# Linear attention and a balanced expert layer: rows of x made inside the first search, first weights asked by the number alone, receptances scaled from PSUM, a fixed order

## The chip, the cores and the metric

The kernel runs on one core of one Trainium2 chip. The metric is the device time in microseconds; the kernel before takes 471.56 us (median of three runs, 471.13 to 471.58). The profile is of one execution, with a span of 470.2 us from its first to its last instruction.

A core has five engines that run side by side and wait for each other by semaphores: TensorE (PE; its weight loads are shown as PEld), VectorE (DVE), ScalarE (ACT), GpSimd (POOL) and SyncE (SP), which here only issues transfers. TensorE writes to PSUM, from where the other engines fetch results.

## The reference

Two blocks follow one another. The first is a recurrent linear attention (batch 4, 8 heads, 768 steps, head size 48), the second a layer of 8 experts to which the 3072 tokens are assigned so that each expert gets exactly 384.

```python
for t in range(S):
    cur = einsum('bhd,bhe->bhde', u * kt, vt)
    y[:, :, t] = einsum('bhd,bhde->bhe', rt, state + cur)
    state = w[:, :, None] * state + einsum('bhd,bhe->bhde', kt, vt)
x = y.transpose(0, 2, 1, 3).reshape(B * S, H * D)          # 3072 rows of 384

logits = x @ w_gate                                        # 3072 x 8
for idx in argsort(-logits.flatten()):                     # best pairs first
    tok, e = idx // E, idx % E
    if assigned[tok] >= 0 or counts[e] >= cap: continue    # cap = 384
    assigned[tok] = e; counts[e] += 1
for e in range(E):
    out[mask_e] = relu(x[mask_e] @ w1[e]) @ w2[e]          # 384 -> 1024 -> 384
```

## The kernel before

Attention goes by 24 units: a batch and a chunk of 128 steps each, four batches side by side, six chunks in turn. Within a unit keys and receptances are scaled by powers of w, so that their products can be taken without a loop over steps. There are two arms: `attention_mild` for decays between 0.7 and 1.2, which a flag read at run time chooses and which the measured inputs take, and `attention_any` for all others.

```python
def scale(n):                                   # a unit: scaled keys, receptances, own term
    load(n + 3)
    kt, rt, vt = loaded.pop(n)
    ks, rs = kss[n % 4], rss[n % 2]
    nc.vector.tensor_mul(ks[:, :, 0:D], heads(kt), heads(wk))
    nc.vector.tensor_mul(rs[:, :, 0:D], heads(rt), heads(wr))
    rk = pool.tile([128, DX], F32, name="rk")
    nc.gpsimd.tensor_mul(rk, rt, kt)
    marks["rk"] = nc.gpsimd.tensor_mul(rk, rk, u_bc).ins
    ...
    nc.vector.tensor_reduce(out=dd, in_=heads(rk), axis=AX.X, op=ALU.add)
    for h in range(H):
        nc.scalar.activation(AT[:, h % 2, h // 2, :], ident, AF.Copy, scale=dd[:, h:h + 1])

def turn(n):                                    # both transposed on TensorE, fetched by ScalarE
    for a in range(HP): nc.tensor.transpose(kT_ps[:, a, :], pair(ks, a), ident)
    for a in range(HP): nc.tensor.transpose(rT_ps[:, a, :], pair(rs, a), ident)
    nc.scalar.copy(kT, kT_ps)
    nc.scalar.copy(rT, rT_ps)

def pairs(n):                                   # products of keys and receptances, masked into AT
    ...
def outputs(n):                                 # y from the state and from AT; the state's update
    ...
def rows(n):                                    # the unit's rows of x, turned back and written to HBM
    xr_ps = ps.tile([128, HP, 128], F32, name="xr_ps")
    for a in range(HP):
        nc.tensor.transpose(xr_ps[:, a, :], turned[n][:, a, :], ident)
    xt = pool.tile([128, DX], F32, name="xt", bufs=3)
    nc.vector.tensor_copy(heads(xt), xr_ps...)
    nc.sync.dma_start(x_dram[ts(b * C + c, 128), :], xt)

for n in range(N):                              # a scheduler decides the order on each engine
    if n + 2 < N: scale(n + 2)
    if n + 1 < N: turn(n + 1); pairs(n + 1)
    outputs(n)
    if n > 0: rows(n - 1)
    if n > 0 and n % B == 0: gate(n // B - 1)   # four units' logits
    ...
gate(C - 1)
rows(N - 1)
```

Then one expert after another is filled. `likely` guesses the level at which an expert is full: three times it counts how many tokens lie above 16 candidates (`count`), then it marks the tokens (`acc`), numbers them (`place`), lists them (`tokens`), and the rows are gathered from HBM. A flag says whether the guess holds; if not, a slow search (`surely`) does it again. The first expert's fill stands after the arms have joined, the others beside the expert before.

```python
def count(self, pool, m, prop, cand, digit_of):
    ind = ...                                   # VectorE: which tokens lie above which candidate
    for j in range(NT // G): nc.tensor.matmul(each, ind..., prop..., ...)
    tt(own, each, self.same, ALU.mult)          # VectorE
    nc.vector.tensor_reduce(out=cnt, ...)
    self.summed = tt(wide, digit_of..., cnt..., ALU.mult)
    nc.tensor.matmul(all_ps, self.ones_h, wide, start=True, stop=True)
    return all_ps

def fill(self, fetch):
    flag = self.likely(**out)
    tok, listed = self.tokens(out["place"])
    got = fetch(tok)                            # three gathers on GpSimd's queue
    found = nc.values_load(flag[0:1, 0:1], ...)
    with self.tc.If(found < 1):
        ...
    self.leave(out["fmax"], out["acc"])
    return out["fmax"], tok, got

def fetch(fmax, tok, xg, late=False):           # after fill: expert number, then its weights
    nc.vector.tensor_scalar(out=number, in0=fmax[0:1, :], ...)
    e = nc.values_load(number[0:1, 0:1], ...)
    nc.sync.dma_start(w1, moe_w1[ds(e, 1)]...)
    ...

ahead = fetch(*walk.fill(rows), late=True)
xT = turn(ahead[0], ahead[-1])                  # gathered rows turned; then w2 is asked
for n in range(E):
    ...
    hid = hidden(w1, xT)                        # h_ps: 24 matmuls of 384 columns, relu
    ...result(n, c, hid, w2, tok)               # o_ps, scattered to the output
```

Of the kernel before, what the change touches and what calls it, by code (L numbers as in the profile page):

```python
# [26 lines left out]
def attention_any(ctx, tc, r, k, v, w, u, wg, x_dram, LG, ident, walk):  # L27
# [16 lines left out]
    lpool = ctx.enter_context(tc.tile_pool(name="a_load", bufs=4))  # L44
    pool = ctx.enter_context(tc.tile_pool(name="a_work", bufs=2))
    ps_t = ctx.enter_context(tc.tile_pool(name="a_ps_t", bufs=2, space=PSUM))
    ps_g = ctx.enter_context(tc.tile_pool(name="a_ps_g", bufs=4, space=PSUM))
    ps_y = ctx.enter_context(tc.tile_pool(name="a_ps_y", bufs=1, space=PSUM))

    NB = 3  # L50
    kpads = [const.tile([128, H, PD], F32, name=f"kpad{i}") for i in range(NB)]
    rpads = [const.tile([128, H, PD], F32, name=f"rpad{i}") for i in range(NB)]
# [64 lines left out]
    ATs, Ks, Rs = [], [], []  # L117
    for i in range(2):
        AT = const.tile([128, H, T], F32, name=f"AT{i}")
        nc.vector.memset(AT, 0.0)  # L120
        ATs.append(AT)
        K = {h: const.tile([128, HP, T], F32, name=f"K{h}_{i}") for h in LEVELS[:-1]}
        R = {h: const.tile([128, HP, 2, PD], F32, name=f"R{h}_{i}") for h in LEVELS}
        for t in (*K.values(), *R.values()):
            nc.gpsimd.memset(t, 0.0)
        Ks.append(K)
        Rs.append(R)
# [137 lines left out]
    walk.constants()  # L265
# [8 lines left out]
    walk.guess(LG, AX.XY, ps_t.tile([128, 128], F32, name="most_ps", tag="t"), ident)  # L274


class Mild:
# [6 lines left out]
    def __init__(self, ctx, tc, r, k, v, w, u, wg, ident):  # L284
# [5 lines left out]
        P2 = 2 * PD  # L290
        E = wg.shape[1]
        M = T // 2
        L = M + 1
        self.tc, self.sources = tc, (k, r, v)
        const = self.const = ctx.enter_context(tc.tile_pool(name="m_const", bufs=1))
        self.lpool = ctx.enter_context(tc.tile_pool(name="m_load", bufs=5))
        self.units = [(b, c) for c in range(C) for b in range(B)]
        self.loaded = {}

        self.vts, self.kss, self.rss = (  # L300
            [const.tile([128, H, PD], F32, name=f"{name}{i}") for i in range(n)]
            for name, n in (("vt", 6), ("ks", 4), ("rs", 2)))
        for t in self.vts + self.kss + self.rss:
            nc.vector.memset(t[:, :, D:PD], 0.0)
        mask = const.tile([128, 128], F32, name="mask_f")
        make_upper_triangular(nc, mask, val=1.0, diag=False)
        self.mask = const.tile([128, 128], U8, name="mask")
        nc.gpsimd.tensor_copy(self.mask, mask)
# [5 lines left out]
        self.wg_sb = const.tile([128, HP, 32], F32, name="wg_sb")  # L314
        nc.vector.memset(self.wg_sb, 0.0)
        flat = w.rearrange("h d -> (h d)")
        wp = const.tile([P2, 8, HP], F32, name="wp")
        nc.vector.memset(wp[:, 0, :], 1.0)
        with nc.allow_non_contiguous_dma(reason="a row to the partitions"):
            for q in range(2):  # L320
                nc.scalar.dma_start(wp[q * PD:q * PD + D, 0, :], w.rearrange("(a q) d -> q d a", q=2)[q])
        row = const.tile([1, DX], F32, name="row")
        nc.sync.dma_start(row, flat.unsqueeze(0))
        self.u_bc = const.tile([128, DX], F32, name="u_bc")
        self.load(0)
        nc.scalar.dma_start(self.u_bc, u.rearrange("h d -> (h d)").partition_broadcast(128))
        for q in range(2):
            nc.scalar.dma_start(self.wg_sb[q * PD:q * PD + D, :, 0:E],
                                wg.rearrange("(a q d) e -> q d a e", q=2, d=D)[q])
        for n in range(1, 3):  # L330
            self.load(n)


        up = const.tile([P2, HP, M + 2], F32, name="up")
        ch = const.tile([P2, HP, T + 2], F32, name="ch")

        nc.vector.tensor_scalar(out=wp[:, 0, :], in0=wp[:, 0, :], scalar1=W_MIN, scalar2=W_MAX,
                                op0=ALU.max, op1=ALU.min)
        nc.vector.memset(up[:, :, 0:1], 1.0)
        nc.gpsimd.memset(ch[:, :, M:M + 1], 1.0)  # L340
        for j in range(7):
            n = 1 << j
            m = min(2 * n, M + 2) - n
            by = wp[:, j, :].unsqueeze(2).to_broadcast([P2, HP, m])
            nc.vector.tensor_mul(up[:, :, n:n + m], up[:, :, 0:m], by)
            m = min(2 * n, M + 1) - n
            by = wp[:, j, :].unsqueeze(2).to_broadcast([P2, HP, m])
            nc.gpsimd.tensor_mul(ch[:, :, L - n - m:L - n], ch[:, :, L - m:L], by)
            nc.vector.tensor_mul(wp[:, j + 1, :], wp[:, j, :], wp[:, j, :])
        nc.vector.reciprocal(ch[:, :, L:T + 2], up[:, :, 1:M + 2])  # L350

        turned = const.tile([P2, HP, T], F32, name="turned")
        nc.scalar.copy(turned, ch[:, :, T + 1:1:-1])
        self.wp, self.scales = wp, []
        with tc.tile_pool(name="m_ps", bufs=2, space=PSUM) as ps, ExitStack() as part:
            for name, t in (("wk", ch), ("wr", turned)):
                sc_ps = ps.tile([128, HP, P2], F32, name="sc_ps")
                for a in range(HP):
                    nc.tensor.transpose(sc_ps[:, a, :], t[:, a, 0:T], ident[0:P2, 0:P2])
                sc = const.tile([128, DX], F32, name=name)  # L360
                nc.scalar.copy(sc.rearrange("p (h d) -> p h d", h=H),
                               sc_ps.rearrange("p a (q d) -> p (a q) d", q=2)[:, :, 0:D])
                self.scales.append(sc)

            pool = part.enter_context(tc.tile_pool(name="mild", bufs=1))
            ge = pool.tile([1, DX], F32, name="ge")
            nc.vector.tensor_single_scalar(out=ge, in_=row, scalar=W_MIN, op=ALU.is_ge)
            both = pool.tile([1, DX], F32, name="both")
            nc.vector.scalar_tensor_tensor(out=both, in0=row, scalar=W_MAX, in1=ge, op0=ALU.is_le, op1=ALU.mult)
            flag = pool.tile([1, 1], I32, name="flag")  # L370
            nc.vector.tensor_reduce(out=flag, in_=both, axis=AX.X, op=ALU.min)
            self.holds = nc.values_load(flag[0:1, 0:1])

    def load(self, n):
        if n >= len(self.units):
            return
        b, c = self.units[n]
        tiles = []
        for name, src in zip(("kt", "rt", "vt"), self.sources):
            H, D = src.shape[1], src.shape[3]  # L380
            if name == "vt":
                t = self.vts[n % len(self.vts)]
                into = t[:, :, 0:D]
            else:
                t = self.lpool.tile([128, H * D], F32, name=name)
                into = t.rearrange("p (h d) -> p h d", h=H)
            self.tc.nc.sync.dma_start(into, src[b, :, ts(c, T), :].rearrange("h s d -> s h d"))
            tiles.append(t)
        self.loaded[n] = tiles


def attention_mild(ctx, tc, mild, r, k, v, w, u, wg, x_dram, LG, ident, walk):
# [19 lines left out]
    const = ctx.enter_context(tc.tile_pool(name="a_const", bufs=1))  # L412
    pool = ctx.enter_context(tc.tile_pool(name="a_work", bufs=2))
    ps = ctx.enter_context(tc.tile_pool(name="a_ps", bufs=1, space=PSUM))

    units, load, loaded = mild.units, mild.load, mild.loaded
    u_bc, wg_sb, wp = mild.u_bc, mild.wg_sb, mild.wp
    wk, wr = mild.scales
    halves = [slice(q * PD, q * PD + PD) for q in range(2)]
    kss, rss, mask, state = mild.kss, mild.rss, mild.mask, mild.state  # L420

    live, turned, marks = {}, {}, {}

    def heads(t):
        return t.rearrange("p (h d) -> p h d", h=H)

    def pair(t, a):
        return t[:, 2 * a:2 * a + 2, :].rearrange("p q d -> p (q d)")

    def scale(n):  # L430
        load(n + 3)
        kt, rt, vt = loaded.pop(n)
        ks, rs = kss[n % 4], rss[n % 2]
        nc.vector.tensor_mul(ks[:, :, 0:D], heads(kt), heads(wk))
        nc.vector.tensor_mul(rs[:, :, 0:D], heads(rt), heads(wr))

        rk = pool.tile([128, DX], F32, name="rk")
        nc.gpsimd.tensor_mul(rk, rt, kt)  # L438
        marks["rk"] = nc.gpsimd.tensor_mul(rk, rk, u_bc).ins  # L439
        dd = pool.tile([128, H], F32, name="dd")  # L440
        nc.vector.tensor_reduce(out=dd, in_=heads(rk), axis=AX.X, op=ALU.add)  # L441
        AT = pool.tile([128, 2, HP, T], F32, name="AT", bufs=3)
        for h in range(H):
            nc.scalar.activation(AT[:, h % 2, h // 2, :], ident, AF.Copy, scale=dd[:, h:h + 1])  # L444
        live[n] = dict(vt=vt, ks=ks, rs=rs, AT=AT)

    def turn(n):

        ks, rs = live[n]["ks"], live[n]["rs"]
        kT_ps = ps.tile([128, HP, T], F32, name="kT_ps")  # L450
        for a in range(HP):
            nc.tensor.transpose(kT_ps[:, a, :], pair(ks, a), ident)
# [87 lines left out]
    for n in range(N):  # L540
        if n + 2 < N:
            scale(n + 2)
# [4 lines left out]
        if n > 0:  # L547
            rows(n - 1)
# [607 lines left out]
```

## Time and profile before

| what | value |
|---|---|
| time, median of three runs | 471.56 us |
| span of the profiled run | 470.2 us |
| TensorE busy | 410.9 us (87%) |
| VectorE busy | 218.4 us (46%) |
| ScalarE busy | 153.3 us (33%) |
| GpSimd busy | 123.4 us (26%) |
| moved by DMA | 54.36 MB, mean 116 GB/s |
| rows of x turned (xr_ps) and written | 24 units, 192 KB each |
| weights | 16 transfers of 1536 KB |

Busy times of different engines overlap. They are averages over stages that differ: attention, the search for the first expert, and the experts. A line of the timeline gives start, duration, engine, source line, operation, output and inputs, how many instructions are merged into it, and in brackets how long the engine had been idle and what ended that. The durations of matmuls overlap, so that the distance from start to start is what a matmul costs.

### The profile page before, as it was taken

How to read it: one execution, taken by the hardware profiler on the slowest of the kernel's cores; microseconds unless marked ns; L12 is line 12 of the kernel's file. 1: busy time of each engine (PE TensorE's matmuls, PEld its weight loads, DVE VectorE, ACT ScalarE, POOL GpSimd, SP SyncE). 2: the span in 40 equal slices, each digit the busy share in tenths (PEclk: the TensorE clock that was granted, in tenths of full speed). 3: DMA queues.
4: the chain of work that ended last, by engine and by line, in shares of the span. 5: the costliest groups of instructions: out<-in, count | busy, mean ns of one | idle time of the engine just before them, and what ended most of it. 6: DMA issues, size and time to landing. Idle time of an engine off the chain costs nothing. (4 is left out here: it accounts for less than half of the span.)

```text
span 470.2 us, 7886 instructions
## 1 busy us (share of the span) xinstructions
PE 410.9 (87%) x2900; PEld 278.1 (59%) x2900; DVE 218.4 (46%) x702; ACT 153.3 (33%) x390; POOL 123.4 (26%) x166
## 2 busy tenths in 40 slices
PE   0499989999999612599999999999999999999994
PEld 0388878888888501255655655555556556556552
DVE  5658778787875484560272371470560640300000
ACT  3658666667676100021220221221121211212200
POOL 2733475456550002020103103112021021301001
PEclk9999999999999955599999999999999999999998
DMA  9747646666641104417007209109018029600000
GB/s 155 114 85 152 137 97 142 137 137 138 150 102 53 59 1 150 171 34 303 33 0 276 95 2 322 48 11 336 23 38 317 18 85 394 206 2 35 17 17 33
DMA packets 93960, 54.36 MB, mean 116 GB/s; under 512 B 77137, under 2 KB 88530, under 8 KB 93906
## 3 DMA queue, kind: packets, MB, share of 16 engines
q1 hardware_dynamic: 88818, 42.48, 32.9%
q0 software_dynamic: 3072, 9.44, 5.9%
q10 hardware_dynamic: 2016, 1.78, 1.3%
q8 instruction: 27, 0.44, 0.4%
q14 instruction: 27, 0.22, 0.2%
HBM read 44.25 MB, written 9.44 MB: 114 GB/s over the span
## 5 line engine op out<-in xcount | busy, mean ns | idle before, releaser
L1103 PE MATMUL h_ps<-xT,w 128*128 128x384 f32 x384 | 135.6, 503 | 0.1
L1110 PE MATMUL o_ps<-w,hid 128*128 128x384 f32 x384 | 128.7, 487 | 0.7
L1110 PEld LDWEIGHTS o_ps<-w,hid 128*128 128x128 f32 x384 | 71.5, 190 | 49.5 <-issue 3.7
L1103 PEld LDWEIGHTS h_ps<-xT,w 128*128 128x128 f32 x384 | 69.7, 193 | 42.4 <-issue 6.3
L1104 ACT ACTIVATE hid<-h_ps 128x384 f32<-128x384 f32 x64 | 31.4, 490 | 108.4 <-PE h_ps L1103 96.5
L1064 POOL DMA_INDIRECT xg<-x_rows,tok x24 | 23.9, 998 | 142.6 <-issue 79.1
L444 ACT ACTIVATE AT<-ident,dd 128x128 f32<-128x128 f32 x192 | 58.8, 392 | 2.4 <-DVE dd L441 2.4
L1113 POOL DMA_INDIRECT out_dram<-o_sb,tok x24 | 23.7, 987 | 133.0 <-ACT o_sb L1112 102.0
L718 DVE TENSOR_TENSOR own<-counts,same 128x64 f32<-128x64 f32 x21 | 4.7, 224 | 93.3 <-PE counts L730 93.3
L1112 ACT COPY o_sb<-o_ps 128x384 f32<-128x384 f32 x24 | 11.5, 479 | 110.3 <-PE o_ps L1110 106.2
L469 PE MATMUL g_ps<-rT,kT 48*128 48x128 f32 x384 | 29.7, 297 | 10.3 <-ACT rT L459 6.5
L438 POOL TENSOR_TENSOR rk<-rt,kt 128x384 f32<-128x384 f32 x24 | 26.0, 1084 | 42.5 <-DMA rt<-in_r_dram 37.4
L472 DVE COPY_PREDICATED AT<-mask,g_ps 128x512 f32<-128x512 uint8 x48 | 32.2, 723 | 8.3 <-PE g_ps L469 8.0
L469 PEld LDWEIGHTS g_ps<-rT,kT 48*128 48x128 f32 x384 | 25.0, 199 | 14.5 <-ACT rT L459 9.6
L489 PE MATMUL y_ps<-AT,vt 128*64 128x128 f32 x384 | 30.5, 281 | 0.0
L492 ACT COPY xT<-y_ps 128x512 f32<-128x512 f32 x24 | 14.0, 585 | 39.8 <-PE y_ps L489 36.8
L439 POOL TENSOR_TENSOR rk<-rk,u_bc 128x384 f32<-128x384 f32 x24 | 25.4, 1061 | 1.6
L489 PEld LDWEIGHTS y_ps<-AT,vt 128*64 128x64 f32 x384 | 25.3, 140 | 0.9 <-issue 0.4
L485 PE MATMUL y_ps<-rT,state 128*64 128x128 f32 x320 | 25.7, 282 | 0.0
L507 POOL TENSOR_TENSOR state<-state,wp 64x192 f32<-64x192 f32 x32 | 18.9, 590 | 14.0 <-DVE state L506 12.8
L1091 ACT COPY xT<-xT_ps 128x384 f32<-128x384 f32 x24 | 10.9, 486 | 32.8 <-PE xT_ps L1090 32.8
L441 DVE TENSOR_REDUCE dd<-rk 128x8 f32<-128x384 f32 x24 | 13.1, 545 | 17.8 <-POOL rk L439 16.1
(171 smaller groups left out, 438.6 us busy)
## 6 DMA issues: line engine op xcount, KB each, us to landing
w<-in_moe_w_dram SPq DMA_DIRECT2D x15, 1536.0 KB, 8.8
kt<-in_k_dram SPq DMA_DIRECT2D x24, 192.0 KB, 3.2
rt<-in_r_dram SPq DMA_DIRECT2D x24, 192.0 KB, 3.6
vt<-in_v_dram SPq DMA_DIRECT2D x24, 192.0 KB, 3.6
x_rows<-xt SPq DMA_DIRECT2D x24, 192.0 KB, 2.2
w<-in_moe_w_dram ACTq DMA_DIRECT2D x1, 1536.0 KB, 8.3
xg<-x_rows,tok POOLq DMA_INDIRECT x24, 5.4
out_dram<-o_sb,tok POOLq DMA_INDIRECT x24, 2.7
```

The source lines that it names most:

```text
L438: nc.gpsimd.tensor_mul(rk, rt, kt)
L439: marks["rk"] = nc.gpsimd.tensor_mul(rk, rk, u_bc).ins
L444: nc.scalar.activation(AT[:, h % 2, h // 2, :], ident, AF.Copy, scale=dd[:, h:h + 1])
L469: g = nc.tensor.matmul(g_ps[:, q, a, :], kT[rows, a, :], rT[rows, a, :], start=True, stop=True)
L472: marks["AT"] = nc.vector.copy_predicated(out=AT[:, q], mask=mask.unsqueeze(1).to_broadcast([128, HP, T]), data=g_ps[:, q]).ins
L485: nc.tensor.matmul(y_ps[halves[q], a, :], S0[:, a, q, :], rT[:, a, :], start=(a == 0), stop=False, skip_group_check=True)
L489: nc.tensor.matmul(y_ps[halves[q], a, :], vt[:, 2 * a + q, :], AT[:, q, a, :], start=(c == 0 and a == 0), stop=(a == HP - 1), skip_group_c ...
L1064: nc.gpsimd.indirect_dma_start(out=xg[:, c, :], out_offset=None, in_=x_dram, in_offset=bass.IndirectOffsetOnAxis(ap=tok[:, c:c + 1], axis=0))
L1103: nc.tensor.matmul(h_ps, w1[:, f, ts(j, 128)], xT[:, f, :], start=(f == 0), stop=(f == KD - 1))
L1104: nc.scalar.activation(hid[:, j, :], h_ps, AF.Relu)
L1110: nc.tensor.matmul(o_ps, hid[:, j, ts(c, 128)], w2[:, j, :], start=(j == 0), stop=(j == KF - 1))
L1113: nc.gpsimd.indirect_dma_start(out=out_rows[n * NC + c], out_offset=bass.IndirectOffsetOnAxis(ap=tok[:, c:c + 1], axis=0), in_=o_sb, in_of ...
```

## The change

It has five parts.

1. The rows of x are no longer made unit by unit. All 24 transposed results stay in SBUF, and their rows are turned and written while the first search waits: two after the first half of each count, three after its second half, five after the selection. Their copy out of PSUM moves from VectorE to ScalarE.
2. The first search stands at the end of the arm, and no longer after the arms have joined. It shares the attention's PSUM banks.
3. The weights w1 are asked as soon as the expert's number is known, ahead of the list of tokens. For the first expert nine multiplications whose result nobody reads stand at the end of the search on TensorE.
4. The receptances are transposed unscaled and multiplied by their scale on the way out of PSUM, by VectorE. That takes the place of a multiplication before (VectorE) and a copy after (ScalarE).
5. The order on the engines is fixed by the program and not by the scheduler. Scale tables are made for w and 1/w side by side, and the first units' work is put ahead of the branch; loads run four units ahead; the search's constants are made three instructions a unit.

The core of the difference (the other arm now reuses buffers of the first one, and is not shown):

```diff
+    def receptances(self, n):
+        rT = self.pool.tile([128, self.r.shape[1] // 2, T], F32, name="rT", bufs=4)
+        self.tc.nc.vector.tensor_mul(rT, self.live[n].pop("rT_ps"), self.wr)
...
-        nc.vector.tensor_mul(rs[:, :, 0:D], heads(rt), heads(wr))
...
-        rT = pool.tile([128, HP, T], F32, name="rT", bufs=3)
-        nc.scalar.copy(rT, rT_ps)
...
-        xT = pool.tile([128, HP, T], F32, name="xT", bufs=6)
+        xT = turned[n] = pool.tile([128, HP, T], F32, name="xT", bufs=N)
...
+    def rows(most):
+        for _ in range(most):
+            ...
+            xr_ps = ps.tile([128, HP, 128], F32, name="xr_ps", tag="y_ps", bufs=2)
+            for a in range(HP):
+                nc.tensor.transpose(xr_ps[:, a, :], turned[n][:, a, :], ident)
+            xt = pool.tile([128, DX], F32, name="xt", bufs=4)
+            nc.scalar.copy(xt.rearrange("p (h d) -> p h d", h=H),
+                           xr_ps.rearrange("p a (q d) -> p (a q) d", q=2)[:, :, 0:D])
+            nc.sync.dma_start(x_dram[ts(b * C + c, 128), :], xt)
+
+    def meanwhile(most):
+        rows(most or N)
+        if not most:
+            spare = ps.tile([128, DX], F32, name="spare", tag="y_ps", bufs=2)
+            for _ in range(9):
+                nc.tensor.matmul(spare, ident, turned[0]..., start=True, stop=True)
...
+    with tc.manual_schedule(engines={nc.tensor.engine, nc.scalar.engine}):
+        with tc.manual_schedule(engines={nc.vector.engine, nc.gpsimd.engine, nc.sync.engine}):
+            mild.rows_turned(1); mild.receptances(1); pairs(0); mild.keys_turned(1)
+            mild.own(1); mild.scale(2); mild.diagonal(1); mild.own(2)
+            for n in range(N):
+                if n + 2 < N:
+                    mild.rows_turned(n + 2); mild.keys_turned(n + 2); mild.receptances(n + 2)
+                ...by_token of the last logits...
+                if n + 3 < N: mild.scale(n + 3)
+                if n + 2 < N: mild.diagonal(n + 2)
+                from_state(n)
+                if n + 1 < N: pairs(n + 1)
+                outputs(n)
+                if n + 3 < N: mild.own(n + 3)
+                if n > 0 and n % B == 0: logits(n // B - 1)
+                ...three of the search's constants...
+            rows(1); logits(C - 1); rows(1); by_token(C - 1); rows(2)
+        first(arm=ctx, bank=..., between=meanwhile)
...
     MEANWHILE = 2, 3, 5
...
             nc.tensor.matmul(each...)              # in count
+        self.between(self.MEANWHILE[0])
...
         nc.tensor.matmul(all_ps...)
+        self.between(self.MEANWHILE[1])
...
         nc.tensor.matmul(st_ps[:, 1, :], self.rest_of, acc, start=True, stop=True)
+        self.between(self.MEANWHILE[2])
...
         nc.tensor.matmul(list_ps..., self.alike, part, start=True, stop=True)
+        self.between(0)
...
+    def search(self, out, ask, fetch):
+        self.likely(out["fmax"], out["acc"], out["place"], out["flag"])
+        ask(out["fmax"])                           # number, then w1 on SyncE's queue
+        self.tokens(out["place"], out["tok"])
+        fetch(out["tok"])
```

## The prediction

> **What bounds the kernel now.** I read the page's slices first, to find the stages; then busy time by stage; then the timeline at the seams. The chain of waits explains only the last 84 us.
>
> ```profile
> PE   0499989999999612599999999999999999999994
> PEclk9999999999999955599999999999999999999998
> ```
>
> Two full stretches of TensorE, with a hole between: attention (slices 2 to 13), the first search (14 to 16), the experts. In the hole the clock is at half.
>
> ```profile
> 120.00:150.00 30.00, 29.87 (x455) 26.07 (x451) 22.04 (x41) 20.51 (x59) 13.28 (x16) 1.00 0.39 96
> 160.00:170.00 10.00, 1.24 (x9) 0.47 (x8) 6.03 (x24) 0.00 (x0) 0.00 (x0) 0.65 0.10 34
> 170.00:180.00 10.00, 1.40 (x13) 0.92 (x13) 7.67 (x35) 0.00 (x0) 0.00 (x0) 0.50 0.01 2
> 190.00:200.00 10.00, 6.18 (x20) 3.09 (x21) 6.08 (x25) 0.48 (x1) 0.00 (x0) 0.50 0.36 124
> ```
>
> Columns: stretch, length, busy us of PE, PEld, DVE, ACT, POOL, then clock, DMA share, GB/s. Attention is bound by TensorE (29.87 of 30), the search by VectorE's chain of small operations, with TensorE free. One unit of attention on TensorE, at full clock:
>
> ```profile
> 83.44 0.60 PE L452 MATMUL kT_ps<-ident,ks 128*128 128x128 f32 x4
> 83.88 0.60 PE L455 MATMUL rT_ps<-ident,rs 128*128 128x128 f32 x4
> 84.41 1.09 PE L485 MATMUL y_ps<-rT,state 128*64 128x128 f32 x16
> 85.33 1.04 PE L489 MATMUL y_ps<-AT,vt 128*64 128x128 f32 x16
> 86.21 0.38 PE L500 MATMUL kv_ps<-vt,ks 128*64 128x48 f32 x6
> 86.54 1.16 PE L469 MATMUL g_ps<-rT,kT 48*128 48x128 f32 x16
> 87.63 0.55 PE L500 MATMUL kv_ps<-vt,ks 128*64 128x48 f32 x10
> 88.11 0.66 PE L516 MATMUL xr_ps<-ident,xT 128*128 128x128 f32 x4
> 88.60 0.60 PE L452 MATMUL kT_ps<-ident,ks 128*128 128x128 f32 x4
> ```
>
> From start to start a unit takes 88.60 - 83.44 = 5.16 us, of which making its row of x (xr_ps) takes 0.49. The seams, from the timeline:
>
> ```profile
> 23.61 2.08 PE L469 MATMUL g_ps<-rT,kT 48*128 48x128 f32 x16 [6.50 <-ACT rT L459]
> ...
> 160.46 0.18 DVE L532 COPY LG<-lg_ps 128x32 f32<-128x32 f32 x1
> ...
> 163.33 0.35 DVE L788 TENSOR_REDUCE m<-LG 128x24 f32<-128x192 f32 x1 [2.69 <-DMA x_rows<-xt]
> ...
> 190.06 0.87 PE L1090 MATMUL xT_ps<-ident,xg 128*128 128x128 f32 x3 [3.14 <-issue]
> ...
> 195.35 1.62 PE L1103 MATMUL h_ps<-xT,w 128*128 128x384 f32 x2
> ```
>
> Attention's products start only at 23.6, behind a copy of rT that stood behind 16 diagonal activations on ScalarE. Logits are complete at 160.64; the search begins 2.7 later, after the last writes of x. The selection (acc) is known at 174.71, the token list at 179.34, the first gather is issued at 180.39, the weights at 182.44, the third gathered tile is turned by 190.93, and the experts run from 195.35 to the end, 274.85 us.
>
> [...] TensorE stops at 160.05, the clock reads 0.51 in the stretch from 163 to 164, and the experts' matmuls stay slow from 195.35 to about 200.5. [...] the rows that now fill the search are transposes. [...] of two weights asked on one queue 0.62 us apart, at 248.86 and 249.48, the first landed after 9.3, the second after 13.2. [...] the trace has 0.72 for a masked copy of that size from PSUM.
>
> **The change part by part.** *Start.* The scale tables' chain loses its slow weight loads in columns (VectorE waited for one until 7.37) and the products no longer wait for two units' diagonals. But in the new order the first receptances wait for a piece of wr that GpSimd copies after four rk products, 1.25 us each, fed by unit 1's loads (issued from 4.39 and 5.37, landing some 3.6 later). So: GpSimd done near 12.2, rT 13.0, keys scaled 13.6, turned and copied 15.4, the mild-decay flag near 15.6, branch and one turn of rows: first product near 18, against 23.6. TensorE is then cold for some 10 us, as before (23.6 to 33.7), so the four units without state finish near 41.5, against 45.0 (the last kv of that group). Gain 3.5.
>
> *Steady.* A unit loses xr: 5.16 - 0.49 = 4.67. Is another engine slower? VectorE per unit: keys 0.68, receptances 0.72, two masked copies 1.45, two state sums 0.69, reduction 0.55: 4.1. ScalarE: 8 diagonals at 0.306, two copies at 0.58: 3.6. GpSimd: 2.1 + 1.2 = 3.3. TensorE remains the bound, and in the fixed order each of its operands is made most of a unit ahead. 16 units x 4.67 = 74.7; the last four, with ever less to turn or pair, 3.9 + 3.9 + 2.9 + 1.9 = 12.6; five sets of logits at 1.25 = 6.2; 1.5 for stalls: 95, from 41.5 to 136.5. Last logits 3.1 (157.55 to 160.64 before): complete at 139.6. Before, 45.0 to 157.55 took 112.5: so 17.5 of the gain are here, 10 from xr and 7 from stalls that the fixed order should remove.
>
> *Search.* The 2.7 us at the seam go. The chain up to acc was 163.33 to 174.71, 11.4. Into each of three counts go two rows, where TensorE waited 0.94, and three, where VectorE works for 1.6: two rows need 1.1, three 1.5 to 2. A row also holds one of four xt buffers for copy 0.5, issue 0.5 and landing 2.1: 0.78 a row, five rows 3.9 against a count's 3.2. So +0.7 three times; faster small matmuls at full clock give 0.4 back: 13.1, acc at 152.7, against 174.71. Gain 22.0.
>
> *Gather.* In the built order SyncE writes 21 rows, then reads the number and asks w1, then writes three rows. The weights go out near acc + 3.5 (they follow the 21st row). 1.5 MB at the 400 GB/s seen from 185 to 193 take 4, plus 2 of latency; the three writes behind them, 1.5: landed at acc + 11. Only then may the gather start; its issues are 1.3 apart, and the third tile is turned by acc + 17.9; before it was 190.93 - 174.71 = 16.2. Loss 1.7. The third gather meets no weights now, and w2 comes later; that is in the figure.
>
> *Experts.* From the third turn to the first expert matmul lie the second search's two counts in the same order: 4.4. Then 274.85, less about 1.2, half of the slow start, since nine idle multiplications keep TensorE busy to about acc + 10.5[...].
>
> Sum: 152.7 + 17.9 + 4.4 + 274.85 - 1.2 = 448.7 span, +1.4 for time over span (471.56 against 470.2) = 450.0.
>
> **Rivals.** *The rows run cold.* If transposes don't keep the clock, a row costs 1.1 (four transposes took 1.09 at the start), two rows 2.2 in a wait of 0.94, five after the selection 5.5 against 2.8: 6 to 10 us more, 456 to 460. [...] Against: the gaps in the new search are short, and ordinary matmuls are mixed in. I give it three in ten; 450 leaves it outside, the upper end holds it.
>
> *The gather isn't held up by w1.* If the three writes slip past the weights, rows are there at acc + 7.5 and the experts start 3 to 4 us earlier: 446. For it: those landings overlap, not strictly one after the other.
>
> *VectorE becomes the bound.* 4.1 against 4.67 is close; operations of 0.56 alone average 0.68 to 0.72 while GpSimd runs, and the search's constants are interleaved. 0.3 us a unit would be 6 in all: 456.
>
> *The start gains as much as it seems.* If TensorE warms sooner, the first product at 18 is worth the whole 5.6: 448.
>
> **Range and chances.** The experts, 275 us, are untouched; all lies in the first 195 us, with about 22 gained. Errors of 3 each at start, steady state, search and gather, partly in common, give about 7: 440 to 459. To be within 2% it must stay above 462, so more than half of the gain would have to fail: faster 0.94, same 0.05, slower 0.01.
>
> **What would show it.** First g_ps near 18; kT_ps to kT_ps about 4.7 in mid-attention with TensorE over 97% busy; LG complete near 140; acc some 13 later; m following LG without a wait for DMA; xr transposes near 0.49 a set if warm, 1.1 if cold; w1 landed before the last x writes, and the gather 6 us after the token list. It is wrong if attention runs at 5.2 a unit (VectorE in TensorE's waits), or if the search takes over 20 us to acc.

## The result, and the profile after

The changed kernel takes 448.01 us (median of four runs, 447.86 to 448.31), the kernel before 471.35 (four runs, 468.01 to 471.58): a ratio of 0.952, with a 95% interval of 0.948 to 0.956. Predicted were 450.0, in a range of 440 to 459. The profiled run has a span of 446.1 us.

The slices of the page (columns as before): the hole between attention and experts now lies in slices 13 to 16, and the low clock in the last two of them.

```profile
PE   2599999999997826999999999999999999999994
PEclk9999999999999966999999999999999999999998
```

Busy time by stage (stretch, length, busy us of PE, PEld, DVE, ACT, POOL, then clock, DMA share, GB/s): attention, the search, the gather, the first expert.

```profile
90.00:110.00 20.00, 20.00 (x339) 17.63 (x335) 17.91 (x39) 15.12 (x45) 13.62 (x20) 1.00 0.67 120
134.00:144.00 10.00, 7.75 (x65) 5.87 (x64) 7.04 (x29) 5.88 (x14) 0.00 (x0) 1.00 0.66 238
160.00:170.00 10.00, 2.83 (x13) 2.04 (x13) 4.85 (x20) 1.44 (x3) 3.16 (x3) 0.50 0.44 127
170.00:180.00 10.00, 8.71 (x27) 4.44 (x28) 7.26 (x36) 0.98 (x2) 0.00 (x0) 0.70 0.25 92
```

TensorE is without a gap in attention, VectorE is at 90%. In the search the clock is at 1.00, with most of TensorE's time spent on transposed rows. The gather still meets an idle, half-clocked TensorE. One unit of attention, on TensorE's timeline:

```profile
87.63 0.66 PE L431 MATMUL rT_ps<-ident,rt 128*128 128x128 f32 x4
88.13 0.60 PE L444 MATMUL kT_ps<-ident,ks 128*128 128x128 f32 x4
88.66 1.09 PE L498 MATMUL y_ps<-rT,state 128*64 128x128 f32 x16
89.68 1.16 PE L488 MATMUL g_ps<-rT,kT 48*128 48x128 f32 x16
90.77 1.09 PE L509 MATMUL y_ps<-AT,vt 128*64 128x128 f32 x16
91.70 0.53 PE L517 MATMUL kv_ps<-vt,ks 128*48 128x48 f32 x16
92.15 0.66 PE L431 MATMUL rT_ps<-ident,rt 128*128 128x128 f32 x4
```

From start to start 92.15 - 87.63 = 4.52 us, against 5.16 before; nothing stands between the groups. The seams, from the timeline of all engines (start, duration, engine, line, operation, and in brackets the idle time before it and what ended it):

```profile
12.45 0.69 DVE L437 TENSOR_TENSOR rT<-rT_ps,wr 128x512 f32<-128x512 f32 x1 [4.42 <-POOL wr L368]
...
17.71 2.08 PE L488 MATMUL g_ps<-rT,kT 48*128 48x128 f32 x16
...
133.18 0.19 DVE L543 COPY LG<-lg_ps 128x32 f32<-128x32 f32 x1 [2.96 <-PE lg_ps L542]
133.41 0.35 DVE L903 TENSOR_REDUCE m<-LG 128x24 f32<-128x192 f32 x1
138.85 0.96 ACT L559 COPY xt<-xr_ps 128x384 f32<-128x384 f32 x2 [1.62 <-DMA x_rows<-xt]
145.49 0.24 DVE L956 SCALAR_TENSOR_TENSOR acc<-em,fmax,past 128x24 bf16<-128x24 f32 x1
149.60 0.41 SPq L1156 DMA_DIRECT2D w<-in_moe_w_dram  x1
150.11 1.47 SPq L561 DMA_DIRECT2D x_rows<-xt  x3
151.11 0.17 DVE L1116 TENSOR_REDUCE tok<-mine 128x3 int32<-128x12 f32 x1
158.36 0.07 DVE L1054 MEMSET sel<- 128x12 uint32 x1 [7.08 <-DMA x_rows<-xt]
160.44 1.18 POOL L1166 DMA_INDIRECT xg<-x_rows,tok  x1 [40.55 <-issue]
164.75 2.47 PE L1225 MATMUL xT_ps<-ident,xg 128*128 128x128 f32 x9 [7.97 <-remote]
171.74 1.62 PE L1238 MATMUL h_ps<-xT,w 128*128 128x384 f32 x2
```

The logits (LG) are there 27.3 us earlier than before, the selection (acc) 29.0 earlier, but the first expert matmul only 195.35 - 171.74 = 23.6 earlier. So over 5 us were won and lost again between acc and h_ps. The list of tokens is there at 151.28; the gather starts 9.2 us later. It starts 1.17 us after the last row's write has landed (159.27), and 1.13 to 1.17 us after it in six other runs whose traces have that landing (1.48 in scheduler). Why that write landed late is seen in the transfers' view, for the writes of x issued just before w1 and for the first one after it (last column: us from issue to landing):

```profile
x_rows<-xt SPq DMA_DIRECT2D x2, 192.0 KB, 1.9
...
x_rows<-xt SPq DMA_DIRECT2D x1, 192.0 KB, 8.1
```

### The profile page after: what moved, and what is told of

Its sections match the earlier page's. It is cut to its first block, busy times and chain, and to the rows that moved or that the text cites. A ratio compares the mean times of both kernels' runs of the same rounds, so it can differ in the third digit from the quotient of the medians.

```text
span 446.1 us, 7907 instructions
## 1 busy us (share of the span) xinstructions
PE 409.2 (92%) x2918; PEld 274.7 (62%) x2918; DVE 206.7 (46%) x675; ACT 154.8 (35%) x390; POOL 122.7 (28%) x170
## 5 line engine op out<-in xcount | busy, mean ns | idle before, releaser
L1166 POOL DMA_INDIRECT xg<-x_rows,tok x24 | 23.6, 984 | 141.0 <-issue 105.9
L1247 ACT COPY o_sb<-o_ps 128x384 f32<-128x384 f32 x24 | 11.5, 480 | 110.3 <-PE o_ps L1245 98.0
L411 POOL TENSOR_TENSOR rk<-rt,kt 128x384 f32<-128x384 f32 x24 | 24.2, 1007 | 22.8 <-DVE dd L418 13.2
L412 POOL TENSOR_TENSOR rk<-rk,u_bc 128x384 f32<-128x384 f32 x24 | 27.9, 1163 | 1.8
L509 PE MATMUL y_ps<-AT,vt 128*64 128x128 f32 x384 | 27.1, 285 | 0.0
L509 PEld LDWEIGHTS y_ps<-AT,vt 128*64 128x64 f32 x384 | 21.2, 140 | 2.9 <-issue 0.2
L447 ACT COPY kT<-kT_ps 128x512 f32<-128x512 f32 x24 | 14.0, 585 | 23.2 <-PE kT_ps L444 23.0
L498 PE MATMUL y_ps<-rT,state 128*64 128x128 f32 x320 | 21.8, 279 | 0.0
L431 PE MATMUL rT_ps<-ident,rt 128*128 128x128 f32 x96 | 17.5, 310 | 4.3 <-DMA rt<-in_r_dram 4.3
L524 POOL TENSOR_TENSOR state<-state,wp 48x192 f32<-48x192 f32 x32 | 16.1, 503 | 18.3 <-DVE state L523 17.0
L444 PE MATMUL kT_ps<-ident,ks 128*128 128x128 f32 x96 | 16.2, 296 | 4.3 <-DVE ks L409 4.3
```

The lines of the kernel that those rows point to most:

```text
L411: nc.gpsimd.tensor_mul(rk, rt[:, :, 0:D], kt)
L412: nc.gpsimd.tensor_mul(rk, rk, self.u_bc.rearrange("p (h d) -> p h d", h=H))
L498: nc.tensor.matmul(y_ps[halves[q], a, :], state[b][:, a, q, :], live[n]["rT"][:, a, :], start=(a == 0), stop=False, skip_group_check=True)
L509: nc.tensor.matmul(y_ps[halves[q], a, :], vt[:, 2 * a + q, :], AT[:, q, a, :], start=(c == 0 and a == 0), stop=(a == HP - 1), skip_group_c ...
L1166: nc.gpsimd.indirect_dma_start(out=xg[:, c, :], out_offset=None, in_=x_dram, in_offset=bass.IndirectOffsetOnAxis(ap=tok[:, c:c + 1], axis=0))
```

## The experiments

To compare runs I use three intervals of each profiled run: from the start to the start of the last LG copy (logits complete); from there to the first h_ps (the first product of the first expert); from there to the end.

| kernel | median us (runs' range) | ratio to before, 95% interval | to LG | LG to h_ps | h_ps to end |
|---|---|---|---|---|---|
| before | 471.35 (468.01 to 471.58) | 1 | 160.46 | 34.89 | 274.85 |
| changed | 448.01 (447.86 to 448.31) | 0.952, 0.948 to 0.956 | 133.18 | 38.56 | 274.36 |
| w1_last | 441.37 (440.28 to 442.72) | 0.941, 0.935 to 0.947 | 130.23 | 34.21 | 274.26 |
| w1_act | 443.17 (440.13 to 444.18) | 0.941, 0.934 to 0.947 | 132.30 | 34.70 | 275.40 |
| rows_in_attention | 450.16 (447.65 to 451.32) | 0.958, 0.952 to 0.965 | 143.95 | 30.37 | 273.98 |
| no_spare | 448.21 (446.78 to 448.88) | 0.954, 0.948 to 0.960 | 132.89 | 39.13 | 275.18 |
| kv_wide | 449.81 (447.12 to 450.50) | 0.957, 0.951 to 0.964 | 134.42 | 38.74 | 274.64 |
| scheduler | 456.70 (456.13 to 458.03) | 0.973, 0.968 to 0.978 | 142.07 | 38.66 | 273.87 |
| recept_sbuf | 461.63 (461.19 to 462.18) | 0.983, 0.978 to 0.988 | 144.14 | 40.27 | 275.09 |
| kt2 | 450.02 (447.29 to 451.45) | 0.955, 0.949 to 0.961 | 136.55 | 38.28 | 274.87 |
| wr_dve | 445.26 (442.04 to 446.01) | 0.946, 0.940 to 0.953 | 130.95 | 38.21 | 273.84 |
| xt8 | 441.50 (439.29 to 442.49) | 0.939, 0.933 to 0.944 | 133.41 | 32.33 | 274.16 |
| best1 | 439.66 (439.12 to 440.06) | 0.935, 0.930 to 0.940 | 130.98 | 32.02 | 275.40 |
| best1_no_spare | 437.61 (437.36 to 438.14) | 0.931, 0.926 to 0.936 | 128.39 | 32.02 | 275.19 |

Differences of up to 3 us in the first of these intervals also come from TensorE's matmuls at the start, which get to full pace (sixteen products in 1.16 us instead of 2.08) at another unit from run to run; the last section shows it. The second of the intervals is free of that. Each ratio is to runs of the kernel before on the same chip: 469.67 us median with w1_last, rows_in_attention, no_spare and kv_wide, 469.43 with scheduler, recept_sbuf, wr_dve and xt8, 470.62 with the other four.

**w1_last: do the last rows wait behind the weights?** My theory after the result: three row writes stand behind 1.5 MB of weights in one queue, and the gather behind them. The rival: the rows themselves end too late.

```diff
-    nc.sync.dma_start(x_dram[...], xt)
+    walk.written = nc.sync.dma_start(x_dram[...], xt).ins
...
-    ask(out["fmax"])
+    with self.tc.issue_after(self.written):   # w1 is asked after the 24th row's write
+        ask(out["fmax"])
```

> The changed kernel, but the first weights are put on SyncE's queue behind the last row of x and not ahead of the last three. Theory A (the three writes stand behind w1 in one queue and land 8.2 us after their issue, so the gather waits until 160.4 though its list is known at 151.3): rows landed near 153, first gather near 153.5, w1 asked near 151.7 and landed near 159, third gathered tile turned near 162, first expert matmul near 166.5: 443 us. Theory B (the gather waits for the end of the arm or for DMA engines that w1 fills whatever the order): gather still near 160, 448 us.

The seam in its timeline:

```profile
147.93 0.17 DVE L1118 TENSOR_REDUCE tok<-mine 128x3 int32<-128x12 f32 x1
148.26 0.41 SPq L1158 DMA_DIRECT2D w<-in_moe_w_dram  x1
150.80 1.18 POOL L1168 DMA_INDIRECT xg<-x_rows,tok  x1 [33.86 <-issue]
157.80 2.12 PE L1227 MATMUL xT_ps<-ident,xg 128*128 128x128 f32 x9 [4.20 <-DMA xg<-x_rows,tok]
```

The gather starts 2.9 us after the list instead of 9.3 (start to start). Of these 6.5 us, 2.7 are given back, since it now runs beside the weights: 7.0 us from its start to the first turn, against 4.3. With 0.2 us less ahead of these steps and 0.4 less behind them, LG to h_ps is 4.35 us shorter. The rest of the 6.6 us between the medians is in the interval to LG, which this edit doesn't touch.

**w1_act: is it the order in the queue, or the load on the transfer engines?**

```diff
-    walk.search(ahead, ask(number, w1), fetch(xg))
+    walk.search(ahead, ask(number, w1, nc.scalar), fetch(xg))   # w1 on ScalarE's queue
```

> The first weights are asked on ScalarE's queue, after 23 of the 24 row copies; the row writes stay on SyncE's queue. Theory (the last rows land late only because they stand behind the weights in one queue): the rows land 2 to 4 us after their issue and the gather is issued about 3 us after the token list: 441 to 444 us. Rival (the 16 engines are simply full with 1.5 MB of weights, whichever queue they came from): the gather is issued 6 us or more after the token list, 446 to 448 us.

```profile
150.10 0.41 ACTq L1156 DMA_DIRECT2D w<-in_moe_w_dram  x1
150.37 0.17 DVE L1116 TENSOR_REDUCE tok<-mine 128x3 int32<-128x12 f32 x1
153.13 1.18 POOL L1166 DMA_INDIRECT xg<-x_rows,tok  x1 [34.12 <-issue]
```

The gather starts 2.8 us after the list. But this run does not part the two theories as it was meant to: the last row's write was issued at 149.82, so all 24 rows, and not 23, went out ahead of the weights. It shows what w1_last shows: rows asked ahead of the weights do not hold the gather. What speaks for the order in one queue are the packets. A row moves in packets of 1.5 KB, the weights in packets of 4 KB; in the changed kernel, whose three late writes are all issued by 151.58, these are the packets from 151.5 to 155.5 and from 155.5 to 159.5:

```profile
DMA packets 313, 1.30 MB, mean 325 GB/s; under 512 B 0, under 2 KB 0, under 8 KB 311
...
DMA packets 503, 0.85 MB, mean 212 GB/s; under 512 B 64, under 2 KB 448, under 8 KB 497
```

No row's packet moves in the first stretch; the second has all of them (448 less 64 is 3 x 128). The gathers, which go through GpSimd's queue, do move among the weights: in w1_last 43 packets of GpSimd's queue beside 98 of SyncE's between 153.5 and 155. So the three writes stood in order behind the weights, and the price of that is 8.1 us to landing instead of 1.9. The load itself costs other queues something too: those gathers landed after 5.0 to 6.8 us, against 3.1 to 3.2 in the changed kernel. A row's write behind the weights in another queue was not tried, so how much of the 8.1 it would keep stays open.

**rows_in_attention: what is the rows' move worth?** Each unit makes the rows of the one before it in the attention again, and one unit's are left for the search.

```diff
             outputs(n)
+            if n > 0:
+                rows(1)
```

> The changed kernel, but each unit's row of x is made in attention, right after the next unit's output, as before the change; nothing is made inside the search. Theory A: TensorE-bound attention grows by 23 x 0.49 = 11, the search up to acc shrinks by 1, the gather starts about 1 us after its list and not 9: 450 us, so that moving the rows is worth only some 2 us as it stands. Rival: the rows fit into waits of attention or the search's stretch costs more than 1: 445 us or less. If moving them is worth their whole TensorE time: 459 us.

```profile
143.95 0.19 DVE L543 COPY LG<-lg_ps 128x32 f32<-128x32 f32 x1 [3.61 <-PE lg_ps L542]
...
155.78 0.41 SPq L1158 DMA_DIRECT2D w<-in_moe_w_dram  x1
159.58 0.17 DVE L1118 TENSOR_REDUCE tok<-mine 128x3 int32<-128x12 f32 x1
160.03 1.18 POOL L1168 DMA_INDIRECT xg<-x_rows,tok  x1 [32.45 <-DVE tok L1118]
```

LG comes 10.8 us later, but the gather starts at 160.03, as in the changed kernel (160.44): without rows behind the weights it waits for the list alone. h_ps is at 174.32, 2.6 later than in the changed kernel. So of 10.8 us won in attention, 8.2 are lost between LG and h_ps, and the main idea of the change is worth 2.2 us as ordered (2.6 by these traces; the ranges of the two kernels' runs overlap). Set against best1 (LG to h_ps in 32.02), the same move would be worth 10.8 - (32.02 - 30.37) = 9.1 us, an estimate from these two runs. Both figures may be too high: without rows in its search the clock has fallen to 0.50 when the nine spare multiplications begin, so that they keep TensorE from 159.19 to 167.76 (8.57 us, against 6.05 in the changed kernel). The first gathered tile, landed at 164.18, is turned behind them at 168.16, the third lands at 168.03. What the kernel would take without them was not tried.

**no_spare: do the nine multiplications keep the clock?**

```diff
-            for _ in range(9):
+            for _ in range(0):
```

> The changed kernel without the nine multiplications at the end of the search. Theory A: they end near 156.8, the clock is at half again from 159, before the first gathered tile is turned at 164.7, so they are worth nothing here: 448 us, difference under 0.5. Rival: they carry some warmth over or hold something up: 450 (or 446) us.

The time is the same. In the changed kernel they run from 150.73 to 156.78 and TensorE then waits 7.97 us; both kernels turn the nine gathered pieces in 2.47 us, the slow form. They do hold the clock, only not long enough: it is 1.00 until 159.0 with them and until 154.1 without (likewise 1.00 from 150 to 155 in best1 and 0.50 in best1_no_spare), but the first turn comes at 164.75.

**kv_wide: the state product with 64 columns, as before the change, and not 48.** The list of the change's parts leaves this difference out.

```diff
-    nc.tensor.matmul(kv_ps[heads[q], a, :], ks[:, 2*a+q, 0:D], vt[:, 2*a+q, 0:D], ...)
+    nc.tensor.matmul(kv_ps[halves[q], a, :], ks[:, 2*a+q, :], vt[:, 2*a+q, 0:D], ...)
```

> The changed kernel, but the state's update multiplies tiles of 64 key columns and writes 64 rows again (48 of them are read), as before the change. Theory A (the quick kv of 0.46 us a unit, against some 0.81 before, comes from the 48 wide tiles): 20 units x 0.35 = 7 us longer, 455 us. Rival (it comes from the order, with kv standing alone behind the output): 448 us.

```profile
87.77 0.62 PE L517 MATMUL kv_ps<-vt,ks 128*64 128x48 f32 x16
...
92.38 0.62 PE L517 MATMUL kv_ps<-vt,ks 128*64 128x48 f32 x16
```

A unit takes 4.61 instead of 4.52 us. Twenty such units make 1.8 us, as measured; I had expected four times that, from the 0.81 us of the kernel before. There other products stand between the state products; the rest of their time goes with the order, then, and not with the width, which leaves the rival right in the main.

**scheduler: what is fixing the order worth?**

```diff
-    with tc.manual_schedule(engines={nc.tensor.engine, nc.scalar.engine}):
-        with tc.manual_schedule(engines={nc.vector.engine, nc.gpsimd.engine, nc.sync.engine}):
+    with nullcontext():
+        with nullcontext():
```

> The two stretches of fixed order in the attention are given back to the scheduler; its order for TensorE differs from the written one only in the first unit. Theory: fixing as such is worth nothing where the order is the same, so within 1 us of the changed kernel, 447 to 449 us. Rival: the fixed order is what brought the earlier end of the attention, then several us more, 452 us or above.

My theory fell: LG comes 8.9 us later, and for two reasons. The first is in the first unit, where TensorE's order differs too:

```profile
24.79 1.32 DVE L490 COPY_PREDICATED AT<-mask,g_ps 128x512 f32<-128x512 uint8 x2
25.61 0.66 PE L509 MATMUL y_ps<-AT,vt 128*64 128x128 f32 x2 [3.98 <-issue]
```

Here VectorE makes the search's constants ahead of the first masked copy, some of them after waiting for GpSimd; in the changed kernel that copy starts at 19.93. TensorE has the first unit's y next, ahead of the second unit's products, and stands idle. The second unit's g_ps starts at 27.41 instead of 23.33 and the third's at 33.82 instead of 29.58: 4.2 of the 8.9 us. The other 4.7 come later. There TensorE's order is the same, but the others' is not. Between 45 and 131 us ScalarE waits longest, 24.2 us for TensorE's y; the next two waits are (us in total, times, longest):

```profile
DVE dd L418 <- POOL rk L412: 16.4, 9, 2.7
POOL rk L411 <- DMA kt<-in_k_dram: 13.4, 8, 3.0
```

The scheduler asks a unit's keys after its receptances and not before, so GpSimd waits for keys and VectorE for GpSimd; TensorE is busy only 18.15 of 20 us from 40 to 60. In the changed kernel neither of these two waits occurs in that stretch. The kernel before had one of them as well: from 45 to 131 its VectorE waited 11.5 us for rk. That the order of the loads carries the 4.7 is read from these waits; a run with that order alone changed was not made.

**recept_sbuf: the receptances scaled in SBUF again.** VectorE multiplies them with a table made token by token (four more transposes), and ScalarE copies rT. To make room, kT has two buffers instead of three, rT three instead of four.

```diff
-    self.tc.nc.vector.tensor_mul(rT, self.live[n].pop("rT_ps"), self.wr)
+    self.tc.nc.scalar.copy(rT, self.live[n].pop("rT_ps"))
...
+    self.tc.nc.vector.tensor_mul(rs[:, :, 0:D], rt[:, :, 0:D], heads(self.wrt))
```

> The receptances are scaled in SBUF again: ScalarE copies rT out of PSUM, VectorE multiplies in SBUF with a table made token by token with four more transposes. Theory (attention is bound by TensorE, at 20.00 us of 20): the unit pitch stays near 4.5 us, only the start may cost 0 to 1.5 us more; 448 to 450 us. Rival (ScalarE, at 15.1 us of 20, is filled by 24 more copies and becomes the bound): up to 24 x 0.58 = 14 us more, about 455 to 462 us.

**kt2: those smaller buffers alone.**

```diff
-    rT = self.pool.tile([...], F32, name="rT", bufs=4)
-    kT = self.pool.tile([...], F32, name="kT", bufs=3)
+    rT = self.pool.tile([...], F32, name="rT", bufs=3)
+    kT = self.pool.tile([...], F32, name="kT", bufs=2)
```

> The changed kernel with two kT buffers instead of three and three rT buffers instead of four, which is what recept_sbuf had as well. Theory A (recept_sbuf lost its 13 us to the scaling in SBUF): within 1.5 us of the changed kernel, 448 to 449.5 us. Theory B (it lost most of them to the buffers taken from it, since ScalarE waited 19 us in all for kT's readers): 455 us or more, unit pitch near 5 us.

recept_sbuf is 13.6 us longer, inside the rival's range and far from the theory's, and kt2 is 2.0 (by LG 3.4), so the scaling, and not the room, is most of it. Of LG's 11.0 us more, 3.7 are at the start (first product at 21.45 instead of 17.71), 3.4 as in kt2, and some 3.9 remain for the steady state. What VectorE pays is in its groups (busy us and mean ns of one), here of recept_sbuf:

```profile
L429 DVE TENSOR_TENSOR rs<-rt,wrt 128x384 f32<-128x384 f32 x12 | 15.5, 1288 | 0.0
L418 DVE TENSOR_TENSOR ks<-kt,wk 128x384 f32<-128x384 f32 x12 | 10.6, 881 | 0.0
```

and of the changed kernel in the same stretch, 60 to 120:

```profile
L409 DVE TENSOR_TENSOR ks<-kt,wk 128x384 f32<-128x384 f32 x13 | 10.5, 809 | 0.0
L437 DVE TENSOR_TENSOR rT<-rT_ps,wr 128x512 f32<-128x512 f32 x13 | 9.0, 691 | 0.6 <-PE rT_ps L431 0.3
```

From SBUF 384 elements take 1288 ns on average, from PSUM 512 take 691 (the prediction reckoned with 0.72 us; a masked copy of 128x512 from PSUM took 723 ns before). But it is not these longer multiplications that hold TensorE up. Its own waits from 45 to 140 in recept_sbuf:

```profile
PE lg_ps L561 <- ACT lgT L556: 4.3, 5, 1.1
PE rT_ps L450 <- DVE rs L429: 0.5, 1, 0.5
```

Five times, once in each set of logits, TensorE waits for ScalarE's copy of the logits, which comes behind copies and diagonals on ScalarE; for VectorE's product it waits once. kt2 has the same wait five times, 1.9 us in total, and the changed kernel has none. So the steady state's loss is in the main ScalarE's queue, as the rival said, though not in every unit: from 52.22 to 65.80 the pitch stays at 4.53. In recept_sbuf's search, 1.9 us longer up to acc, ScalarE waits 2.42 us for a row buffer instead of 1.62, and the clock is at 0.50 from 152.8 to 156.2; how the 1.9 divide is not shown.

**wr_dve: the wait at the start.**

```diff
-    nc.gpsimd.tensor_copy(self.wr[:, :, M + 1:T], ...)
+    nc.vector.tensor_copy(self.wr[:, :, M + 1:T], ...)
```

> The second piece of the table wr is copied by VectorE instead of GpSimd. Theory (the start is gated by GpSimd's copy, 4.42 us of VectorE's wait ahead of the first scaling): first g product at 14 to 15.5 us instead of 17.7, and all that follows 2 to 3 us earlier, 445 to 446 us. Rival (the next wait, for keys or for the clock, takes its place): first product earlier, but the end of the attention within 1 us, 448 us.

First product at 15.96 instead of 17.71 (14 to 15.5 were expected), LG 2.2 earlier, median 2.75 less. The wait was the gate, as the theory had it; of the 2.2, the first product's start accounts for 1.75, and the rest lies within what TensorE's pace at the start varies by (up to 3 us in LG, last section).

**xt8: the row buffers.**

```diff
-    xt = pool.tile([128, DX], F32, name="xt", bufs=4)
+    xt = pool.tile([128, DX], F32, name="xt", bufs=8)
```

> Eight row buffers instead of four. Theory (in the search ScalarE waits 1.6 and 1.3 us for row buffers whose writes are under way): acc about 1.4 us earlier. The last rows still go behind the first weights in the queue, so the gather gains about as much, 1 to 3 us: 445 to 447 us. Rival (the count of the search waits for something else): 448 us.

It won more than twice what I expected. From LG to acc 10.76 us instead of 12.31, for the waits of ScalarE (the 1.62 in the line at 138.85) are gone; and in the order as built all 24 rows now stand ahead of the weights, against my theory, and the gather starts 3.4 us after the list. LG to h_ps is 6.2 shorter. So this one number does what w1_last does, and takes the hold in the search away too.

**best1 and best1_no_spare: together.** Eight buffers, w1 after the last row, wr on VectorE; the second without the spare multiplications.

> Eight row buffers, the first weights asked after the last row, wr's second piece on VectorE, together. Theory: the start gains 2 to 2.7 us, the search 1.5, and the gather is issued 2 to 4 us after the token list instead of 9.2; since eight buffers alone already let the rows go ahead of the weights (441.5 us), the sum is 441.5 less 2.7: 438.5 to 439.5 us. Rival (the earlier start is lost again at the next wait): 441 us.

> As best1, without the nine spare multiplications. Theory (the gap to the first gathered tile is some 8 us either way once the last count is over, longer than the spares bridge): within 0.7 us of best1. Rival (now that the gather comes early, the spares keep the clock up to the first gathered tile): 1 to 2.5 us more than best1, with the turns at 2.5 us for nine instead of 2.1 to 2.2 and more cold matmuls after them.

From LG to h_ps both take 32.02 us, so the spare multiplications do nothing here either; TensorE turns the gathered pieces slowly in both (2.47 us for nine). In best1 they miss by little: the clock falls at 155.7, the first turn is at 156.01. In w1_last and xt8 it falls just after the first turn (near 158.2 and 159.3, the turns at 157.80 and 159.02), and nine take 2.12 and 2.20. best1_no_spare is 2.05 us faster, outside what the theory and its rival allowed, all of it before LG, where the two don't differ (128.39 against 130.98): its products got to 1.16 us one unit earlier. I don't take that for an effect of the edit; nothing here shows a way from the one to the other. The gain that is certain is the one of LG to h_ps (6.5 us) and of the first product's start (1.9); the median goes from 448.0 to 439.7, a ratio to before of 0.935.

## Why the prediction was right

The total is right within 2 us, but three of its steps were off by more, in opposite directions, so that this closeness is partly luck.

| step | predicted us | measured us | off |
|---|---|---|---|
| four units without state done | 41.5 | 39.05 | -2.5 |
| from there to LG complete | 98.1 | 94.3 | -3.8 |
| LG to acc complete | 13.1 | 12.4 | -0.7 |
| acc to third tile turned | 17.9 | 21.5 | +3.6 |
| third turn to h_ps | 4.4 | 4.5 | +0.1 |
| h_ps to end of span | 273.65 | 274.36 | +0.7 |
| time over span | 1.4 | 1.8 | +0.4 |

The offsets sum to -2.2 us; 450.0 - 2.2 = 447.8.

*Start: mechanism right, size wrong.* The first product is at 17.71 (predicted 18), and behind the copy of wr on GpSimd, as said. But I let only 3.5 of the 5.6 us through. TensorE's matmuls did run slow for 10 to 12 us, as before (sixteen products in 2.08 us instead of 1.16, from 17.71 to about 29.3, against 23.61 to 33.3), and just for that reason the whole shift came through: 45.0 - 39.05 = 5.9. The rival "the start gains as much as it seems" had the size right and the reason wrong, for TensorE did not warm sooner. Other runs with the same instructions here were at full pace within some 5 us (last section), and then this step ends up to 3 us earlier: its size is luck in part.

*Steady state: right.* 4.52 a unit against 4.67: 16 x 0.15 = 2.4 of the 3.8; narrower state products give 0.09 a unit. TensorE waits for nothing, as the 20.00 of 20 show, so the 1.5 us for stalls were not needed. The 7 us "from stalls that the fixed order should remove" are gone; that the fixed order removed them is shown for some 4.7, which come back in the units after the second when the order is given back (4.2 more come back in the first). As idle time only part of the 7 can be seen: in the kernel before TensorE was busy 108.76 of the 112.5 us from 45.0 to 157.5. The rival "VectorE becomes the bound" is false at 17.9 of 20, and in recept_sbuf too it is ScalarE that TensorE waits for.

*Search: right.* +0.7 a count for the buffers was the term of 2.1 us; taking the hold away (xt8) gives 1.55. No wait at the seam: m follows LG by 0.2 us.

*The rows run cold: false.* Eight transposes took 1.11 us at 145.83, about half a microsecond a set against the 1.1 of a cold one, and the clock is at 1.00 to 158. The rival's assumption, that transposes don't keep the clock, is not borne out in this mix, with small matmuls every 1.2 to 2.6 us from 134 to 146. The clock did fall in one search: in recept_sbuf TensorE waits 2.12 us for a copy of ScalarE until 151.86 and is busy only 1.28 us from 149.4 to 152.8; from 152.8 to 156.2 the clock is 0.50, and twelve transposes take 2.69 us instead of 1.92; then it is back at 1.00. No run shows transposes alone.

*Gather: right in kind, too small.* The order (21 rows, weights, three rows) and w1 at acc + 3.5 (measured 3.9) hold. "Landed at acc + 11" is the term that failed: the third write is issued near 151.1 and lands 8.2 us later, at 159.27, which is acc + 13.5. Of the 2.5 us, 0.4 are the weights' issue. The two us before the stream flows were in my step: 117 and 123 GB/s from 149.6 to 151.6. After that it ran at 225 to 414 GB/s in the six microseconds to 157.6, 334 on average and not 400: 2112 KB, which are 2.16 MB, take 6.5 us at that rate and not 5.5, so 1.0 is from there. The rest, 1.2 (the figures are rounded), lies between the end of the stream and the rows' landing, and I have no cause for it. Another 1.2 us lie between the last landing and the gather's start, for which my step had nothing. So the gather came 9.2 us after the list and not 6. The rival "the gather isn't held up by w1" is false: w1_last, w1_act and xt8 each take the hold away, and LG to h_ps falls by 4.4, 3.9 and 6.2 us.

*Experts: no warm start.* I credited the spare multiplications with 1.2 us. They end at 156.78; the first turn is at 164.75, in part because the gather came 3.7 us later than my step had it (acc + 14.7, not + 11), and the clock reads 0.50 from 160. Measured: 0.5 us, and taking the nine away costs nothing that can be told.

## What to carry to other kernels

A transfer that is asked early is only worth its place if nothing small that is needed sooner stands behind it in the same queue (here a row's write behind w1 landed 8.1 us after its issue, one ahead of it 1.9 us after): look for the last small write before each large load, and either order it first or give it enough buffers to have gone already. (Whether another queue for the load would do was not settled here, since w1_act changed the order too.) When a stage is moved into another's waits, follow the gain to the next join: here 10.8 us won in attention became about 2 at the end, since another wait ended at the same time. And when judging what fixing the order does, compare the queues of the transfers and of the engines that feed the bound, not only the bound's own, and look at the first unit as well as at the steady ones.

## What the runs showed that I had not expected

**TensorE's pace at the start.** The same instructions at nearly the same times took different times in different runs. The second and third groups of products in the timeline of best1:

```profile
21.47 2.08 PE L488 MATMUL g_ps<-rT,kT 48*128 48x128 f32 x16
...
27.05 1.16 PE L488 MATMUL g_ps<-rT,kT 48*128 48x128 f32 x16
```

and of best1_no_spare, whose first product is at 15.81 as well:

```profile
20.98 1.16 PE L488 MATMUL g_ps<-rT,kT 48*128 48x128 f32 x16
24.47 1.16 PE L488 MATMUL g_ps<-rT,kT 48*128 48x128 f32 x16
```

One is at full pace within some 5 us of its first product, the other after some 8 to 11; it moves LG by 2.6 us, and in w1_last by some 3. The granted clock reads 1.00 from 12 to 30 us in both all the same: that TensorE is slow is read from the sixteen products, 2.08 us and then 1.16, and why it is slow is not shown. The four runs of w1_last alone took 440.28, 440.36, 442.37 and 442.72. Edits of one or two us must be read from intervals inside the trace, not from medians here.

**Two operands from SBUF.** In recept_sbuf VectorE's product of 384 elements at 87.36, begun 0.08 us after GpSimd's rk (1.02 us), took 1.36. At 98.63, begun 0.03 after GpSimd's, it took 0.55, and GpSimd's took 1.44. Each time one of the two took longer, once VectorE's and once GpSimd's. In the changed kernel the product of 512 elements from PSUM at 89.47, begun 0.14 after GpSimd's rk, took 0.69, and rk 1.01: neither took longer. From 40 to 120 all 17 of these took 0.69; of recept_sbuf's 16 products of receptances in SBUF, the 14 beside GpSimd's rk took 1.35 to 1.37 and the two beside none 0.55 and 0.59. So scaling on the way out of PSUM also spared VectorE a product that took 1.35 us and more beside GpSimd's; why the two slow each other is not shown.

**Gathering beside a large load.** From the gather's start to the first turn it takes 4.3 us where the weights have landed (changed kernel), 5.7 to 7.0 in w1_act, best1, xt8 and w1_last. (In rows_in_attention it takes 8.1, but there the spare multiplications stand in front of the turn.) In w1_last, xt8 and best1 the first turn comes 9.0 to 9.8 us after w1 was asked, about when w1 lands (9.5 and 9.1 us in the first two); that the landing of w1 sets it was not tried.
